# Products of keys and x four at a time in 64x64 tiles of the array, in two stretches a batch

## The chip, the cores and the metric

The program runs on one core of one Trainium2 chip. The time is the device time of one execution in microseconds. The kernel before took 803.41 us in the median of three runs (803.13, 803.41 and 806.71).

A core has five instruction streams that run side by side, each in its own order: TensorE (PE: matrix products; loading its weights is listed apart as PEld), VectorE (DVE), ScalarE (ACT), GpSimd (POOL) and SyncE (SP, which here only issues transfers). They meet at semaphores. Transfers (DMA) are issued by SP, and for v and z by POOL.

## The reference, cut to what matters

Two stages over 8 batches of 3200 rows, 256 wide. The first is a gated attention without softmax:

```
attn = maximum(z @ z.T / 3200, 0) ** 2
x    = u * (attn @ v)                       # per batch 3200 x 256
```

The second mixes rows through a hidden width of 64. As an outer product over rows, it needs no 3200 x 3200 matrix:

```
wq, wk = x @ w_q, x @ w_k                   # 3200 x 64 each
W_tok  = wq @ wk.T / 8
mixed  = W_tok @ x  =  wq @ (wk.T @ x) / 8
out    = maximum(mixed, 0) @ w_out
```

The change is about `wk.T @ x`, a sum over all 3200 rows of a batch that gives 64 x 256 numbers. The kernel calls wk the keys and this product the heads.

## The kernel before, in words

The kernel takes a batch's 3200 rows in 25 tiles of 128, and these in seven groups: six of four tiles (512 rows) and one of a single tile (`LASTG`). For each group it makes

- scores (`scores`, line 223): two row tiles at a time, with 64 rows of contraction each, so that one product uses the upper and the other the lower half of the array;
- their relu (`first_stage`, on DVE line 246 or ACT line 242) and square (`second_stage`, on POOL line 261 or ACT line 259). Because z @ z.T is symmetric, part of the squares is transposed by DMA (line 281) instead of being computed again;
- the second product with v (`second_product`, line 302), the bulk of TensorE's work: 10,000 matmuls with 64 rows of contraction, again one on each half of the array, summed in four PSUM banks (`acc`);
- the gate (`gate`): ACT copies one half's sum into `both` (line 318), DVE adds the other (line 319), POOL multiplies by u into `x_sb` (line 334), and a DMA transposes x (`turn_x`, line 348).

A group's x then goes through the second stage. `use_keys` runs `projections` (line 365: wq and wk together), ACT casts them to `qk` (line 378), and a DMA transposes `qk` into `kx` (`turn_keys`, line 383), so that keys lie with rows on partitions. Two POOL copies double the keys (`double_keys`, line 395), because `heads` (line 402) loads 128 columns of weights: the 64 keys twice, so that the 64 x 256 result appears on both halves of the partitions, where `mix` wants it. For each of a group's tiles there is one matmul on the upper 64 rows of the array and one on the lower, into two banks. They ride in the same PSUM slot as the projections of a later group, right behind them, and DVE adds both banks into `ha` (line 417). After a batch's last group DVE adds the two parts to `hs` (line 424). Then `mix` (line 430), relu on ACT into `rt` (line 447), `proj` with w_out (line 457, the full 128 rows of the array), scaling on ACT into `fo` (line 485) and the store to memory (line 486).

What sets the order: the kernel is scheduled by hand (`manual_schedule`). A planner at build time keeps a clock for each engine, for SP and for the transfers, with fixed costs, and writes the instructions out in the order that comes from it. Within each engine this order is final. `acc` work fills TensorE; everything else (scores, keys, heads, mix, proj) is slipped in when one of two PSUM slots (`ps`, two banks each) is free. `move` hands a transfer to SP with a ready and a due time; `at_time` runs something when the planner's clock gets there.

At the end of the run the last two groups of the last batch are not projected first: their part of the heads comes from x.T @ x (`last_gram`, line 500, and `last_heads`, line 510), and is added to the rest (lines 952 and 959) before the last batch's `mix`.

Of the kernel before, what the change touches and what calls it, by code (L numbers as in the profile page):

```python
# [16 lines left out]
def kernel(  # L17
# [35 lines left out]
    NX = 6  # L53
# [7 lines left out]
    pk = ctx.enter_context(tc.tile_pool(name="pk", bufs=3))  # L61
# [3 lines left out]
    psum = ctx.enter_context(tc.tile_pool(name="psum", bufs=3))  # L65
# [20 lines left out]
    zT, vs, us, xs, xTs, qks, ks, hacc, hss, rts, zds = ({} for _ in range(11))  # L86
# [274 lines left out]
    def projections(b, gi, ps, stop=True):  # L361
        n = min(2, widths[gi] // P)
        for c in range(NC):
            for r in halves(gi):
                nc.tensor.matmul(  # L365
                    out=ps[:, r, 0 : n * P],
                    lhsT=wqk[top(r), c, :, :].rearrange("p t h -> p (t h)"),
                    rhs=xTs[b, gi][top(r), 0:n, c, :],
                    start=(c == 0),
                    stop=(stop and c == NC - 1),  # L370
                )
# [16 lines left out]
    doubled = set()  # L388

    def double_keys(b, gi):  # L390
        doubled.add((b, gi))
        nn = widths[gi] // P
        for r in halves(gi):
            sl = slice(2 * r, min(2 * r + 2, nn))
            nc.gpsimd.tensor_copy(out=ks[b, gi][:, sl, r, :], in_=ks[b, gi][:, sl, 1 - r, :])  # L395

    def heads(b, gi, ps, begun=()):
        nn = widths[gi] // P
        assert (b, gi) in doubled
        for n in range(nn):  # L400
            for r in range(2):
                nc.tensor.matmul(  # L402
                    out=ps[:, r, D : 2 * D],
                    lhsT=ks[b, gi][top(r), n, :, :].rearrange("p a h -> p (a h)"),
                    rhs=x_rows(b, gi, n)[top(r), :, :],
                    start=(n == 0 and r not in begun),
                    stop=(n == nn - 1),
                )
        del xs[b, gi]

    def heads_out(b, gi, ps):
        part = ps[:, 0:2, D : 2 * D]
        if gi == 0:
            hacc[b] = psml.tile([P, 2, D], FP32, tag="ha", name="ha")
            nc.vector.tensor_copy(out=hacc[b][:], in_=part)
        else:
            nc.vector.tensor_add(out=hacc[b][:], in0=part, in1=hacc[b][:])  # L417
# [113 lines left out]
    keys_at, out_of, turned_at, z_at = {}, {}, {}, {}  # L531
# [88 lines left out]
    def double(b, gi):  # L620
        keys_at[b, gi] = give(POOL, clock[PE], 0.6) + 0.5
        double_keys(b, gi)

    def use_keys(b, gi):
        open_slot()
        ps = ps_tile("qk")
        prior = None
        if keyed and keys_at.get(keyed[0], 1e9) <= clock[PE]:
            prior = keyed.pop(0)
        projections(b, gi, ps, stop=not prior)  # L630
        clock[PE] += 0.44 if gi < LASTG else 0.24
        if prior:
            heads(*prior, ps, halves(gi))
            clock[PE] += 0.44 if prior[1] < LASTG else 0.11
# [6 lines left out]
            lambda t: at_time(t, lambda: double(b, gi)),  # L641
        )
        if prior:
            heads_out(*prior, ps)
            done = give(DVE, done, 0.7)
            if prior[1] == LASTG:
                done += 0.4
# [5 lines left out]
        if (b, gi) == (last, LASTG - 2):  # L653
            for _ in keyed:
                add_extra(done + 4.0, "heads", use_heads)

    def use_heads():
        open_slot()
        ps = ps_tile("hd")
        prior = keyed.pop(0)  # L660
        heads(*prior, ps)
        clock[PE] += 0.44 if prior[1] < LASTG else 0.11
        heads_out(*prior, ps)
        done = give(DVE, clock[PE] + FROM_PE, 0.7)
        if prior[1] == LASTG:
            heads_known(prior[0])
        close_slot(done)

# [197 lines left out]
    while groups or work or current["left"]:  # L866
# [9 lines left out]
                and (x[1] != "keys" or len(keyed) < 2 or keys_at.get(keyed[0], 1e9) <= now)  # L876
                and (x[1] != "proj" or len(stored) < 2 or stored[-2] <= now)
                and (x[1] != "heads" or keys_at.get(keyed[0], 1e9) <= now)
# [26 lines left out]
    while extras or later or moves:  # L905
        x = next((x for x in extras if x[1] == "proj"), None)
        if not x:
            ripe = [
                x
                for x in extras  # L910
                if x[1] not in ("keys", "heads")
                or (x[1] == "keys" and len(keyed) < 2)
                or keyed[0] in doubled
            ]
            ripe += [x for x in moves if not x[6] or x[6]()]
            x = min(later + ripe, key=lambda x: x[0])
# [9 lines left out]
    while keyed:  # L926
        use_heads()
# [22 lines left out]
    hsum = psml.tile([P, D], FP32, tag="hm", name="hm", bufs=1)  # L950
    ha = hacc.pop(last)
    nc.vector.tensor_add(out=hsum[:], in0=ha[:, 0, :], in1=ha[:, 1, :])
# [6 lines left out]
    nc.vector.tensor_add(out=hss[last][:], in0=psl[:, 0:D], in1=hsum[:])  # L959
# [45 lines left out]
```

## Time and profile before

| | |
|---|---|
| median of the runs shown | 803.41 us |
| profiled execution: its span, the only time given for it | 804.1 us |
| TensorE busy | 774.2 us (96%), 12,373 matmuls |
| POOL busy | 627.2 us (78%) |
| ACT busy | 579.3 us (72%) |
| DVE busy | 467.7 us (58%) |
| transfers | 141.54 MB, 309,356 packets |

A row of a group of instructions gives line, engine, operation, output and inputs, shapes and count, then the busy time and the mean duration of one, then the idle time of the engine just before them. A row of the timeline gives the start in us, the length in us of the run of like instructions, the engine, and in brackets how long the engine had been idle and whom it waited for. Matmuls overlap: one lasts 0.27 us from its start to the end of its last result, while the next start much sooner. What a matmul costs TensorE is therefore the distance from start to start, which a long run of like matmuls gives.

### The profile page before, as it was taken

The page shows a single profiled execution, that of the slowest core. Times are in us where ns is not written, and L with a number is a line of the kernel's source. Part 1 is how long each engine was busy: PE and PEld are TensorE (multiplying, and loading weights), DVE is VectorE, ACT ScalarE, POOL GpSimd, SP SyncE. Part 2 cuts the span into 40 slices and gives each one's busy share as a digit, 9 for nine tenths or more (in the row PEclk, how much of TensorE's full clock was granted, in tenths as well). Part 3 has the DMA queues.
Part 4 walks back from the last instruction along what each step waited for, and adds up shares of the span by engine and source line. Part 5 has one row for each costly group of instructions (what it writes and reads, how often), then busy time and mean ns, then how long its engine had stood idle before and what let it go on. Part 6 is the DMA issues. An engine that isn't in the chain of part 4 may idle for free.

```text
span 804.1 us, 28204 instructions
## 1 busy us (share of the span) xinstructions
PE 774.2 (96%) x12373; PEld 657.3 (82%) x12373; DVE 467.7 (58%) x485; ACT 579.3 (72%) x690; POOL 627.2 (78%) x512
## 2 busy tenths in 40 slices
PE   7989999997999999999999999999999999999985
PEld 4879899886888888988888788988889788888863
DVE  4665567553666556755576555765557655564424
ACT  5766888774896777877676768777777676887714
POOL 7887878875788878898878878878877887888730
PEclk9999999999999999999999999999999999999998
DMA  7999999999999988999999989999799998787425
GB/s 188 149 159 174 179 179 156 163 170 192 196 160 206 222 159 166 160 219 196 188 161 186 197 173 200 170 193 201 183 179 162 195 220 165 152 165 171 120 48 216
DMA packets 309356, 141.54 MB, mean 176 GB/s; under 512 B 287728, under 2 KB 290672, under 8 KB 309232
## 3 DMA queue, kind: packets, MB, share of 16 engines
q1 hardware_dynamic: 302320, 123.55, 80.4%
q0 software_dynamic: 6768, 15.98, 14.8%
q8 instruction: 97, 1.59, 0.9%
q14 instruction: 27, 0.22, 0.1%
q10 hardware_dynamic: 144, 0.20, 0.1%
HBM read 59.64 MB, written 26.21 MB: 107 GB/s over the span
## 4 chain that ended last, share of the span: by engine, by line
PE 89%; DVE 4%; DMA 2%; ACT 2%; issue 1%; POOL 1%; POOLq 0%; SPq 0%; DVEq 0%; ACTq 0%
PE acc L302 64%; PE sc L223 12%; PE fo L457 6%; PE qk L365 3%; PE qk L402 2%; DVE g L246 2%; PE mx L430 1%; DMA out_dram<-fo 1%; DMA v_sb<-in_v_dram 1%; DVE hs L424 1%; DVE ha L417 1%; POOL at L261 1%; DVE both L319 1%; ACT both L318 0%; DMA z<-in_z_dram 0%
## 5 line engine op out<-in xcount | busy, mean ns | idle before, releaser
L302 PE MATMUL acc<-v_sb,at 64*128 64x256 f16 x7312 | 495.9, 270 | 4.1 <-DVE both L319 2.5
L261 POOL TENSOR_TENSOR at<-g 128x1024 f16<-128x1024 f32 (+1 forms) x238 | 442.7, 1872 | 72.6 <-DVE g L246 63.3
L302 PEld LDWEIGHTS <-at 64*128 64x128 f16 x7312 | 394.2, 94 | 65.3 <-issue 10.8
L246 DVE TENSOR_SCALAR g<-sc 128x1024 f32<-128x1024 f32 (+1 forms) x285 | 333.9, 1189 | 132.9 <-PE sc L223 118.8
L259 ACT ACTIVATE at<-g 128x1024 f16<-128x1024 f32 (+2 forms) x230 | 233.9, 1026 | 16.6 <-DVE g L246 13.0
L242 ACT ACTIVATE g<-sc 128x1024 f32<-128x1024 f32 x183 | 184.9, 1012 | 60.4 <-PE sc L223 59.3
L334 POOL TENSOR_TENSOR x_sb<-both,u_sb 128x512 f16<-128x512 f32 (+1 forms) x112 | 134.5, 1206 | 72.4 <-DVE both L319 70.4
L223 PE MATMUL sc<-zT 64*128 64x512 f16 x920 | 178.5, 379 | 4.6 <-DVE g L246 3.9
L302 PE MATMUL acc<-v_sb,tt 64*128 64x256 f16 x2304 | 162.2, 269 | 0.0
L319 DVE TENSOR_TENSOR both<-acc,both 128x512 f32<-128x512 f32 (+1 forms) x104 | 69.2, 670 | 136.3 <-ACT both L318 131.4
L302 PEld LDWEIGHTS <-tt 64*128 64x128 f16 x2304 | 123.9, 94 | 11.7 <-issue 0.2
L318 ACT COPY both<-acc 128x512 f32<-128x512 f32 (+1 forms) x104 | 58.1, 564 | 42.8 <-PE acc L302 40.9
L223 PEld LDWEIGHTS <-zT 64*128 64x128 f16 x920 | 57.7, 94 | 18.6 <-issue 14.8
L485 ACT ACTIVATE fo<-fo 128x1024 f32<-128x1024 f32 (+2 forms) x50 | 45.4, 909 | 34.1 <-PE fo L457 27.6
L447 ACT ACTIVATE rt<-mx 128x1024 f16<-128x1024 f32 (+1 forms) x49 | 45.7, 934 | 23.1 <-PE mx L430 23.0
L378 ACT CAST qk<-qk 128x512 f16<-128x512 f32 (+1 forms) x54 | 29.4, 545 | 36.7 <-PE qk L402 28.1
L457 PE MATMUL fo<-wo,rt 128*128 128x256 f16 x400 | 53.4, 274 | 1.2 <-ACT rt L445 0.6
L457 PEld LDWEIGHTS <-rt 128*128 128x128 f16 x400 | 34.7, 98 | 15.8 <-issue 9.8
L417 DVE TENSOR_TENSOR ha<-qk,ha 128x512 f32<-128x512 f32 x38 | 26.2, 690 | 33.2 <-ACT qk L378 33.0
L365 PE MATMUL qk<-xT_sb,wqk 64*128 64x256 f16 (+1 forms) x404 | 32.1, 265 | 0.0
L402 PE MATMUL qk<-x_sb,kx 64*128 64x256 f16 x368 | 29.6, 269 | 0.0
L395 POOL COPY kx<-kx 128x128 f16<-128x128 f16 (+1 forms) x101 | 26.1, 288 | 3.0 <-DMA kx<-qk 3.0
(44 smaller groups left out, 225.4 us busy)
## 6 DMA issues: line engine op xcount, KB each, us to landing
u_sb<-in_u_dram SPq DMA_DIRECT2D x48, 512.0 KB, 4.8
out_dram<-fo SPq DMA_DIRECT2D x45, 512.0 KB, 4.8
v_sb<-in_v_dram POOLq DMA_DIRECT2D x35, 320.0 KB, 6.1
zn<-in_z_dram POOLq DMA_DIRECT2D x7, 400.0 KB, 5.9
tt<-at SPq DMA_TRANSPOSE x144, 4.2
out_dram<-fo SPq DMA_DIRECT2D x6, 256.0 KB, 2.1
u_sb<-in_u_dram SPq DMA_DIRECT2D x8, 128.0 KB, 3.3
out_dram<-fo SPq DMA_DIRECT2D x8, 128.0 KB, 2.5
```

The costliest lines, as they stand in the source:

```text
L223: nc.tensor.matmul(out=sc[:, h, 0:gw], lhsT=zT[b][top(h), ts(ti, P)], rhs=zT[b][top(h), ds(gs, gw)], start=True, stop=True,)
L242: nc.scalar.activation(out=g[:, hs, 0:w], in_=sc[:, hs, 0:w], func=RELU, scale=GSCALE)
L246: nc.vector.tensor_scalar(out=g[:, hs, 0:w], in0=sc[:, hs, 0:w], scalar1=0.0, scalar2=GSCALE, op0=AOP.max, op1=AOP.mult,)
L259: nc.scalar.square(out=out, in_=g[:, hs, 0:w])
L261: nc.gpsimd.tensor_mul(out=out, in0=g[:, hs, 0:w], in1=g[:, hs, 0:w])
L302: nc.tensor.matmul(out=accs[half, r][:, ds((j % 2) * D, D)], lhsT=weights(b, gi, ti, j)[top(r), :], rhs=vs[b][top(r), ti, :], start=(first ...
L318: nc.scalar.copy(out=both[:, 0 : n * D], in_=accs[half, 0][:, 0 : n * D])
L319: nc.vector.tensor_add(out=both[:, 0 : n * D], in0=accs[half, 1][:, 0 : n * D], in1=both[:, 0 : n * D])
L334: nc.gpsimd.tensor_mul(out=xs[b, gi][:, 0:n, :, r, :].rearrange("p n c d -> p (n c) d"), in0=both[:, 0 : n * D].rearrange("p (m d) -> p m ...
L365: nc.tensor.matmul(out=ps[:, r, 0 : n * P], lhsT=wqk[top(r), c, :, :].rearrange("p t h -> p (t h)"), rhs=xTs[b, gi][top(r), 0:n, c, :], st ...
L447: nc.scalar.activation(out=out, in_=ps[:, 0:nr, 0 : ND * n * P], func=RELU)
L457: nc.tensor.matmul(out=banks[r][:, ds(j * D, D)], lhsT=flat[:, ds((dc * n + j) * P, P)], rhs=wo[:, dc, :], start=(dc == 0 and j == 0), sto ...
```

## The change

- `heads` multiplies the 64 keys only once: the weights are 64 rows by 64 columns. Even tiles of the stretch write partitions 0 to 63 of the result, odd tiles partitions 64 to 127; in each case one matmul takes the upper and one the lower 64 rows. Four matmuls in a row thus name four different quarters of the array. There are as many matmuls as before (390), each with 256 columns of x.
- Heads no longer ride behind projections. They run in a PSUM slot of their own, in two stretches a batch: one for groups 0 to 2 (24 matmuls), one for groups 3 to 6 (26; in the last batch groups 3 and 4, 16). `keys_landed` starts a stretch when the keys of all its groups are there by the planner's clock.
- `double_keys` and its 101 POOL copies are gone.
- The sum is now split: even tiles on the upper partitions, odd tiles on the lower, two banks each. DVE copies the first stretch's banks to `ha`, adds the second stretch's, and adds the two banks (lines 406, 409 and 410 of the new kernel). Two transfers of 64 x 256 numbers (64 KB each) on SP's queue then carry each half of the partitions to the other (`cross_heads`), and DVE adds what arrives (`heads_done`): for the last batch in place, to be used by the last addition to `hs`.
- `mix` of a batch is planned from the moment at which the crossed halves have landed.
- Buffers: x 7 instead of 6, keys 5 instead of 3, `both` 2 instead of 3; a transposition of keys is issued only while one of the five is free.

The rest of the order is worked out anew by the planner.

```diff
-    NX = 6
+    NX = 7
+    NK = 5
-    pk = ctx.enter_context(tc.tile_pool(name="pk", bufs=3))
+    pk = ctx.enter_context(tc.tile_pool(name="pk", bufs=NK))
-    psum = ctx.enter_context(tc.tile_pool(name="psum", bufs=3))
+    psum = ctx.enter_context(tc.tile_pool(name="psum", bufs=2))
...
-    def double_keys(b, gi):
-        doubled.add((b, gi))
-        nn = widths[gi] // P
-        for r in halves(gi):
-            sl = slice(2 * r, min(2 * r + 2, nn))
-            nc.gpsimd.tensor_copy(out=ks[b, gi][:, sl, r, :], in_=ks[b, gi][:, sl, 1 - r, :])
-
-    def heads(b, gi, ps, begun=()):
-        nn = widths[gi] // P
-        assert (b, gi) in doubled
-        for n in range(nn):
+    def heads(b, gis, ps):
+        todo = [(gi, n) for gi in gis for n in range(widths[gi] // P)]
+        for i, (gi, n) in enumerate(todo):
             for r in range(2):
                 nc.tensor.matmul(
-                    out=ps[:, r, D : 2 * D],
-                    lhsT=ks[b, gi][top(r), n, :, :].rearrange("p a h -> p (a h)"),
+                    out=ps[top(i % 2), r, 0:D],
+                    lhsT=ks[b, gi][top(r), n, 1 - n // 2, :],
                     rhs=x_rows(b, gi, n)[top(r), :, :],
-                    start=(n == 0 and r not in begun),
-                    stop=(n == nn - 1),
+                    start=(i < 2),
+                    stop=(i >= len(todo) - 2),
                 )
...
+    def heads_out(b, ps):
+        if b not in hacc:
+            hacc[b] = psml.tile([P, 2, D], FP32, tag="ha", name="ha", bufs=1)
+            nc.vector.tensor_copy(out=hacc[b][:], in_=ps[:, :, 0:D])
         else:
-            nc.vector.tensor_add(out=hacc[b][:], in0=part, in1=hacc[b][:])
-        if gi == LASTG:
-            heads_done(b)
+            ha = hacc[b]
+            nc.vector.tensor_add(out=ha[:], in0=ps[:, :, 0:D], in1=ha[:])
+            nc.vector.tensor_add(out=ha[:, 0, :], in0=ha[:, 0, :], in1=ha[:, 1, :])
+
+    def cross_heads(b, r):
+        if r == 0:
+            hx[b] = psml.tile([P, D], FP32, tag="hx", name="hx", bufs=1)
+        nc.sync.dma_start(out=hx[b][top(r), :], in_=hacc[b][top(1 - r), 0, :])
 
     def heads_done(b):
-        hss[b] = psml.tile([P, D], FP16, tag="hs", name="hs")
-        ha = hacc.pop(b)
-        nc.vector.tensor_add(out=hss[b][:], in0=ha[:, 0, :], in1=ha[:, 1, :])
+        if b < B - 1:
+            hss[b] = psml.tile([P, D], FP16, tag="hs", name="hs")
+            nc.vector.tensor_add(out=hss[b][:], in0=hacc.pop(b)[:, 0, :], in1=hx.pop(b)[:])
+        else:
+            ha = hacc[b]
+            nc.vector.tensor_add(out=ha[:, 1, :], in0=ha[:, 0, :], in1=hx.pop(b)[:])
...
+    FIRST_HEADS = range(3)
+
+    def keys_landed(b, gi):
         keyed.append((b, gi))
-        if len(keyed) == 2 and gi == LASTG:
-            add_extra(done + 14.0, "heads", use_heads)
+        for gis in FIRST_HEADS, range(3, NG if b < last else LASTG - 1):
+            if gi in gis and all((b, i) in keyed for i in gis):
+                add_extra(clock[PE] + 0.5, "heads", lambda gis=gis: use_heads(b, gis))
+
+    def use_heads(b, gis):
         open_slot()
         ps = ps_tile("hd")
-        prior = keyed.pop(0)
-        heads(*prior, ps)
-        clock[PE] += 0.44 if prior[1] < LASTG else 0.11
-        heads_out(*prior, ps)
+        heads(b, gis, ps)
+        clock[PE] += 0.2 + 0.0547 * sum(widths[gi] // P for gi in gis)
+        heads_out(b, ps)
         done = give(DVE, clock[PE] + FROM_PE, 0.7)
-        if prior[1] == LASTG:
-            heads_known(prior[0])
         close_slot(done)
+        if gis is FIRST_HEADS:
+            return
+        done = give(DVE, done, 0.35)
+        move(done + SLACK, done + 2.0, 0.55, 0.1, lambda: cross_heads(b, 0))
+        move(
+            done + SLACK, done + 2.0, 0.55, 0.1, lambda: cross_heads(b, 1),
+            lambda t: at_time(t, lambda: crossed(b)),
+        )
+
+    def crossed(b):
+        heads_done(b)
+        give(DVE, clock[PE], 0.35)
+        if b < last:
+            heads_known(b)
```

More of the change, by code (lines that the diff above doesn't have):

```diff
@@ L84 @@
     ctx.enter_context(tc.manual_schedule())
-    zT, vs, us, xs, xTs, qks, ks, hacc, hss, rts, zds = ({} for _ in range(11))
+    zT, vs, us, xs, xTs, qks, ks, hacc, hx, hss, rts, zds = ({} for _ in range(12))
     def rows(t, b):
@@ L369, in projections @@
                     start=(c == 0),
[L370 removed]
+                    stop=(c == NC - 1),
                 )
@@ L626, in use_keys @@
         ps = ps_tile("qk")
-        prior = None
-        if keyed and keys_at.get(keyed[0], 1e9) <= clock[PE]:
-            prior = keyed.pop(0)
-        projections(b, gi, ps, stop=not prior)
+        projections(b, gi, ps)
         clock[PE] += 0.44 if gi < LASTG else 0.24
-        if prior:
-            heads(*prior, ps, halves(gi))
-            clock[PE] += 0.44 if prior[1] < LASTG else 0.11
         ready = clock[PE] + FROM_PE
@@ L907 @@
         if not x:
[L908 to L916, printed above, removed]
+            ripe = [x for x in moves if not x[6] or x[6]()]
+            x = min(later + extras + ripe, key=lambda x: x[0])
         clock[PE] = max(clock[PE], x[0])
```

39 lines of the change are left out of this document (6 added, 33 removed).

## The prediction

> **What bounds the kernel now.** I read the page first, then TensorE's waits, the chain of work that ended last, and timeline windows. The page's head and the chain by engine:
>
> ```profile
> span 804.1 us, 28204 instructions
> PE 774.2 (96%) x12373; PEld 657.3 (82%) x12373; DVE 467.7 (58%) x485; ACT 579.3 (72%) x690; POOL 627.2 (78%) x512
> PE 89%; DVE 4%; DMA 2%; ACT 2%; issue 1%; POOL 1%; POOLq 0%; SPq 0%; DVEq 0%; ACTq 0%
> q1 hardware_dynamic: 302320, 123.55, 80.4%
> ```
>
> TensorE is busy almost all the time and carries 89% of the chain. Its longest waits (total, times, longest) are few:
>
> ```profile
> PE mx L430 <- ACT fo L485: 4.5, 1, 4.5
> PE sc L223 <- DVE g L246: 3.9, 6, 1.0
> PE hd L402 <- POOL kx L395: 2.9, 1, 2.9
> ```
>
> So work taken from TensorE's stream between start and tail should shorten the span one for one, and work taken from POOL or DVE should not. Three rows of the chain give a batch and a matmul:
>
> ```profile
> 247.76 1.97 PE acc L302 x36
> 342.96 1.97 PE acc L302 x36
> 761.36 11.73 PE acc L302 x213
> ```
>
> The first two are the same place in two batches: one batch takes 95.2 us, over some 12373/8 = 1547 matmuls, 0.0616 us each with all waits. The third: (11.73 - 0.27)/212 is close to 0.054 us a 64-row matmul, so 0.109 a pair on the two halves of the array (0.0545 below).
>
> **The heads before, and a change of tiling.** A window of the timeline near the end:
>
> ```profile
> 746.21 1.05 PE L457 MATMUL fo<-wo,rt 128*128 128x256 f16 x8
> 747.19 0.39 PE L302 MATMUL acc<-v_sb,at 64*128 64x256 f16 x4
> 756.12 1.91 PE L302 MATMUL acc<-v_sb,tt 64*128 64x256 f16 x32
> 757.96 0.39 PE L457 MATMUL fo<-wo,rt 128*128 128x256 f16 x2
> 758.29 0.61 PE L365 MATMUL qk<-xT_sb,wqk 64*128 64x256 f16 x8
> 758.74 0.60 PE L402 MATMUL qk<-x_sb,kx 64*128 64x256 f16 x8
> 759.17 0.38 PE L302 MATMUL acc<-v_sb,at 64*128 64x256 f16 x4
> ```
>
> Eight head matmuls take 759.17 - 758.74 = 0.43 us, at the usual rate, with no loss on either side. A change to the full array and back costs something: eight fo take 0.98, two take 0.33, so each is 0.108 and the way back 0.11; the way there is 1.84 - 32 x 0.0545 = 0.10. The 64x64 tiles are a tiling that the trace doesn't show. For their change I take the nearest rows, 0.10 each way. Bounds: 0 (only columns are divided anew) and 0.21 each way, twice what is shown.
>
> **TensorE's sum.** Up to the last keys of the last batch, the heads before are 7 x 25 + 12 = 187 pairs: 187 x 0.109 = 20.4 us. After, the same 374 matmuls run in 15 stretches. If four share the time of two now, that is 93.5 rounds x 0.109 = 10.2; if not at all, 20.4. The nearest evidence is the pair: two 64-row matmuls of 256 columns take what one fo of 128 rows takes (0.109 against 0.108), so independent parts of the array run together without loss. I take 10.2. The changes of tiling add 15 x 2 x 0.10 = 3.0 (0 to 6.3). Net -7.2 us; ends -10.2 and +6.3.
>
> Against the full gain speaks the loading of weights, one load for each matmul:
>
> ```profile
> L402 PEld LDWEIGHTS <-kx x390: 92/94/136, 79.9 to 779.2; 64*128 64x128 f16 x195
> 784.48 0.30 PEld L510 LDWEIGHTS hl<-G,wk 128*128 128x128 f32 x2 [0.94 <-ACT G L955]
> L510 PEld LDWEIGHTS hl<-G,wk x4: 186/188/189, 783.2 to 784.6; 128*128 128x128 f32 x4
> ```
>
> The f32 loads last 188 ns against 94, and the second begins 0.30 - 0.19 = 0.11 us behind the first. If 64-column loads went at that slower rate, each would occupy 0.055: two behind each other for each half of the rows fit a round of 0.109; four behind each other make it 0.22. The Trainium skill, "TensorEngine Tiling (Array Packing)", Restrictions, says that column tiling disables the fast weight load; "TensorE: Matmul & The Clock Gate", LDWEIGHTS, gives columns / 1.2 GHz for a load, 53 ns for 64. By those rules with one path for all loads, the sum would be the second rival's. No run shows a 64-column load; the f32 row agrees with the rate.
>
> **Off TensorE.** Rows of the costliest groups:
>
> ```profile
> L246 DVE TENSOR_SCALAR g<-sc 128x1024 f32<-128x1024 f32 (+1 forms) x285 | 333.9, 1189 | 132.9 <-PE sc L223 118.8
> L417 DVE TENSOR_TENSOR ha<-qk,ha 128x512 f32<-128x512 f32 x38 | 26.2, 690 | 33.2 <-ACT qk L378 33.0
> L395 POOL COPY kx<-kx 128x128 f16<-128x128 f16 (+1 forms) x101 | 26.1, 288 | 3.0 <-DMA kx<-qk 3.0
> ```
>
> POOL loses 26.1 us. DVE loses 54 operations of 0.69 for 16 such and some of half the size, and in the new order takes 26 more relus of 1.2 from ACT, which evens out. All three stay under 80% busy and hidden behind TensorE: nothing. Projections no longer hold their slot for DVE's addition; the 3.9 us of waits for slots is all that this could give, and 16 extra slots take some back: nothing net. `both` with two buffers waits for the products of the gate before last; at the tightest place (the tail below) POOL ends them at 773.72 and ACT copies at 776.12: nothing while those 2.4 us hold.
>
> The 16 crossing transfers are 1 MB beside 141.5 and 16 issues on SP, in front of transpositions queued behind them. Prices of an issue and a landing come from 64 KB loads:
>
> ```profile
> L183 SPq DMA_DIRECT2D wk<-in_moe_w_k_dram x4: 472/606/1438, 21.5 to 35.8; - x4
> DMA to landing us min/median/max: 2.4/3.0/6.5
> ```
>
> Two issues delay SP by 1.2 us a batch, within what a transposition has in hand (rival three). DVE's last addition stands some 90 to 200 matmuls (5.5 to 12 us) behind the crossing in the written order, against a landing of 3.0: hidden, except in the tail, and at 6.5 a DVE wait of 1 us, with relu work queued behind it.
>
> **The tail.** The last keys hold up the end:
>
> ```profile
> 771.95 1.77 POOL L334 TENSOR_TENSOR x_sb<-both,u_sb 128x512 f16<-128x512 f32 x1 [7.43 <-DVE both L319]
> 774.72 1.19 SPq L383 DMA_TRANSPOSE kx<-qk  x1
> 776.01 4.37 SPq L348 DMA_TRANSPOSE xT_sb<-x_sb  x2
> 776.12 0.37 ACT L318 COPY both<-acc 128x256 f32<-128x256 f32 x1 [1.43 <-PE acc L302]
> 777.03 1.64 POOL L334 TENSOR_TENSOR x_sb<-both,u_sb 128x256 f16<-128x256 f32 x2 [1.34 <-DVE both L319]
> 778.62 0.52 POOL L395 COPY kx<-kx 128x128 f16<-128x128 f16 x2
> 778.97 0.86 PE L402 MATMUL hd<-x_sb,kx 64*128 64x256 f16 x8 [2.93 <-POOL kx L395]
> 783.25 0.70 PE L510 MATMUL hl<-G,wk 128*128 128x256 f32 x2 [0.19 <-DVE G L954]
> ```
>
> Without the earlier heads the cast starts 0.44 sooner, and without copies the heads start when keys land: at 776.6 to 778.0 (landing 2.3 to 3.6 after 774.72, less 0.44) instead of 778.97. But DVE must then add twice (1.1 us), the crossing waits on SP behind the last transposition of x, issued by about 780, and lands 3.0 later, near 783.5; and DVE's copy for the last product with w_k is queued behind the addition that waits for it, two operations of some 0.4 (a little over half of 0.69, for half the size): 784.3 instead of 783.25. I take +1.0; ends -1.0 (the crossing hidden) and +3.0 (it lands last behind both transpositions).
>
> **One stall.** The single long wait, in the second batch:
>
> ```profile
> 180.34 8.14 DMA out_dram<-fo
> 188.56 0.38 ACT L485 ACTIVATE fo<-fo 128x256 f32<-128x256 f32 x1 [6.39 <-DMA out_dram<-fo]
> 188.99 0.61 PE L430 MATMUL mx<-qk,hs 64*128 64x256 f16 x4 [4.51 <-ACT fo L485]
> 189.37 2.57 PE L302 MATMUL acc<-v_sb,at 64*128 64x256 f16 x22
> ```
>
> A scaling waits 6.39 us for its buffer, as the store is late, and TensorE waits 4.51. Then 22 matmuls take 2.57 instead of 1.4, mx 0.38 instead of 0.22, with the next ones slow too: some 6.1 in all. In the new order the stores of that batch are queued 148 or more matmuls ahead of the scaling that needs the buffer, against 138 here: 0.6 us more, not 6.39. I keep the stall.
>
> **The sum.** 804.1 - 20.4 + 10.2 + 3.0 + 1.0 = 797.9. The profiled execution is 0.7 above the median 803.4, so 797.2. Its own ends, with a change of tiling at 0 to 0.15 us and the tail at -1 to +3: 792.2 to 800.7.
>
> **Rivals.** (1) The stall goes too: the batch's mix comes later, so stores meet other transfers. 797.2 - 6.1 = 791.1. For it: it happens in one batch of seven. Against: the early loads, and a margin hardly larger.
>
> (2) Slower: four loads go one behind the other. Rounds of 0.22 give 93.5 x 0.22 = 20.6, nothing is saved, and changes and tail stay: 804.1 + 0.2 + 3.0 + 1.0 - 0.7 = 807.6. It decides from a round of 0.174 on, where (20.4 - 4.0)/93.5 is used up. Speaking for it is the f32 row; against it, that pairs run together. The plainer form, that the quarters don't run together, ends at the same time.
>
> (3) TensorE waits for keys. Formerly they lay ready for a group; now each stretch follows its last transposition by as little as 108 matmuls (6.6 us), ten of them by under 8 us. Landing is:
>
> ```profile
> L383 SPq DMA_TRANSPOSE kx<-qk x54: 1182/1254/2805, 61.9 to 774.7; - x54
> DMA to landing us min/median/max: 2.3/4.0/7.7
> ```
>
> At the median 2.6 us are in hand, at 7.7 none. Behind TensorE stand acc matmuls that need none of it. With 0.5 us on average at ten places: 802.2. At 0.6 a place the gain is gone.
>
> **How the numbers follow.** A measurement of this kernel can tell about 0.5% (4 us) from no change: faster ends below 799.4, slower begins at 807.4. Forecast 0.48 (0.44 faster, 0.04 same). Stall gone 0.22 (faster). Loads in a row 0.14 (0.07 same, 0.07 slower, as 807.6 sits on the bound). Waits for keys 0.16 (0.02 faster, 0.11 same, 0.03 slower). Faster 0.68, same 0.22, slower 0.10. The range takes in the stall's going and the waits, and leaves out most of rival two: 789.5 to 805.0.
>
> **What would show it.** Right: 24 head matmuls take 0.65 to 0.7 us, four starting together every 0.11, with 0.1 lost at either end; a batch takes 94.2 instead of 95.2; the tail from keys to the w_k product is about 1 us longer. Wrong: rounds of 0.2; rows where hd waits for kx, or DVE for hx; a wait of mx or fo for a store, new or gone.

## The result

The new kernel takes 792.04 us in the median (790.96 to 793.60, four runs) against 805.06 us for the old one beside it (803.13 to 807.06, four runs): ratio 0.987, interval 0.983 to 0.992. It is faster, by 1.3%. On another chip, where both were run again more often, it took 792.77 us (six runs) against 800.96 (17 runs, 797.9 to 805.3): ratio 0.990, interval 0.987 to 0.993. The old kernel varies more from run to run than the new one, and the first chip caught it at the long end. The gain to be explained is therefore 8 us rather than 13; the forecast was 6.2 us (797.2 against 803.4, a ratio of 0.992).

Head of the page of the new kernel, and its chain by engine. Its profiled execution took 790.96 us of device time with a span of 789.2; that of the old one had a span of 804.1.

```profile
span 789.2 us, 28159 instructions
PE 763.2 (97%) x12373; PEld 645.7 (82%) x12373; DVE 479.4 (61%) x479; ACT 551.8 (70%) x659; POOL 612.9 (78%) x418
PE 91%; DVE 3%; DMA 2%; issue 1%; ACT 1%; POOL 1%; SPq 0%; DVEq 0%; POOLq 0%; ACTq 0%
```

TensorE has as many matmuls as before and is busy 11.0 us less. POOL has 94 instructions fewer. Three of TensorE's waits (total, times, longest):

```profile
PE hl L509 <- DVE G L936: 5.1, 1, 5.1
PE sc L224 <- DVE g L247: 3.1, 5, 0.8
PE hd L393 <- DMA kx<-qk: 0.6, 1, 0.6
```

The 4.5 us in which `mx` waited for a store are gone. In their place the tail has a wait of 5.1 us for `G`, where a wait of 2.9 us for the key copies stood. Waits for keys, the third rival, come to 0.6 us, once, in the tail.

Two stretches of heads in TensorE's timeline, with the row that follows each:

```profile
378.92 0.85 PE L393 MATMUL hd<-x_sb,kx 64*64 64x256 f16 x24
379.70 1.05 PE L456 MATMUL fo<-wo,rt 128*128 128x256 f16 x8
...
419.91 0.95 PE L393 MATMUL hd<-x_sb,kx 64*64 64x256 f16 x26
420.80 0.39 PE L303 MATMUL acc<-v_sb,at 64*128 64x256 f16 x4
```

From the start of a stretch to the start of what follows, 24 matmuls take 0.78 us and 26 take 0.89. At the old rate of 0.0545 a matmul they would have taken 1.31 and 1.42. The single records show why: four matmuls start 3 to 4 ns apart, and the next four begin 0.099 us after the last of them, 0.123 us the first time. Taken over the 15 stretches, the last matmul ahead of a stretch is 0.093 us longer than the last of a pair usually is, and the last of a stretch 0.096 longer than the last of four: that is the change of tiling.

The weight loads, first in the new kernel and then in the old (count, then busy time and mean ns of one):

```profile
L303 PEld LDWEIGHTS <-at 64*128 64x128 f16 x7312 | 393.0, 94 | 66.8 <-issue 12.7 <-ACT g L243 2.0
L393 PEld LDWEIGHTS <-kx 64*64 64x64 f16 x390 | 9.7, 106 | 4.6 <-issue 3.7 <-DMA kx<-qk 0.9
```

```profile
L402 PEld LDWEIGHTS <-kx 64*128 64x128 f16 x390 | 21.3, 94 | 4.6 <-POOL kx L395 3.2
```

A load of 64 columns lasts 106 ns, longer than one of 128 columns with 94. But 390 x 0.106 = 41 us of loads fill only 9.7 us of time: some four go on at once. In the old kernel 390 x 0.094 = 37 us filled 21.3, not quite two at once.

**Where the time went.** Between 60 us from the span's start and the start of the last `acc` matmul I summed two things over TensorE's records: the time from the start of each head matmul to the start of the next matmul, and all that the other matmuls took beyond their usual distance (acc 0.0547, sc 0.108, qk and mx 0.054, fo 0.109). The second sum holds waits, slow clock and changes of tiling; the ways into the head stretches, 15 x 0.093 = 1.4 us, are in it.

| profiled execution | heads, us | all else beyond the usual, us |
|---|---|---|
| before | 21.0 | 24.1 |
| before, two more profiles | 21.0, 21.0 | 22.9, 20.3 |
| after | 12.4 | 17.8 |
| after, once more | 12.6 | 17.7 |

Heads and their ways in go from 21.0 to 13.8, so -7.2 us; 0.4 of that is eight matmuls that now stand behind the last `acc` matmul. All else goes from 24.1 to 16.4, so -7.7 us. From the last `acc` matmul to the end it is 28.29 before and 28.45 after, +0.16. Together -14.7 of the 14.9 us between the two spans. The forecast had the first, and +1.0 for the third; for the second it had nothing.

### The profile page after: what moved, and what is told of

Same layout as the page of the kernel before. It is cut to its first block, busy times and chain, and to the rows that moved or that the text cites. A ratio compares the mean times of both kernels' runs of the same rounds, so it can differ in the third digit from the quotient of the medians.

```text
span 789.2 us, 28159 instructions
## 1 busy us (share of the span) xinstructions
PE 763.2 (97%) x12373; PEld 645.7 (82%) x12373; DVE 479.4 (61%) x479; ACT 551.8 (70%) x659; POOL 612.9 (78%) x418
## 4 chain that ended last, share of the span: by engine, by line
PE 91%; DVE 3%; DMA 2%; issue 1%; ACT 1%; POOL 1%; SPq 0%; DVEq 0%; POOLq 0%; ACTq 0%
PE acc L303 66%; PE sc L224 12%; PE fo L456 6%; PE qk L366 3%; DVE g L247 2%; PE hd L393 1%; PE mx L429 1%; DVE both L320 1%; DMA v_sb<-in_v_dram 1%; DMA hx<-ha 1%; ACT both L319 1%; POOL x_sb L335 1%; DVE ha L410 0%; DMA z<-in_z_dram 0%; SPq L349 0%
## 5 line engine op out<-in xcount | busy, mean ns | idle before, releaser
L262 POOL TENSOR_TENSOR at<-g 128x1024 f16<-128x1024 f32 (+2 forms) x245 | 451.5, 1858 | 82.5 <-DVE g L247 66.5
L247 DVE TENSOR_SCALAR g<-sc 128x1024 f32<-128x1024 f32 (+2 forms) x309 | 363.9, 1197 | 153.0 <-PE sc L224 137.6
L260 ACT ACTIVATE at<-g 128x1024 f16<-128x1024 f32 x223 | 229.4, 1036 | 30.7 <-DVE g L247 27.2
L243 ACT ACTIVATE g<-sc 128x1024 f32<-128x1024 f32 (+1 forms) x159 | 159.2, 1003 | 60.5 <-PE sc L224 59.8
L303 PE MATMUL acc<-v_sb,tt 64*128 64x256 f16 x2304 | 158.7, 269 | 0.0
L224 PEld LDWEIGHTS <-zT 64*128 64x128 f16 x920 | 56.8, 94 | 17.6 <-issue 12.4
L366 PEld LDWEIGHTS <-wqk 64*128 64x128 f16 x416 | 22.8, 94 | 2.5 <-issue 0.5
L303 PE MATMUL acc<-v_sb,ttl 64*128 64x256 f16 x384 | 24.6, 269 | 0.0
L303 PEld LDWEIGHTS <-ttl 64*128 64x128 f16 x384 | 19.7, 94 | 3.5 <-issue 0.8
```

What stands on the lines that cost most here:

```text
L224: nc.tensor.matmul(out=sc[:, h, 0:gw], lhsT=zT[b][top(h), ts(ti, P)], rhs=zT[b][top(h), ds(gs, gw)], start=True, stop=True,)
L243: nc.scalar.activation(out=g[:, hs, 0:w], in_=sc[:, hs, 0:w], func=RELU, scale=GSCALE)
L247: nc.vector.tensor_scalar(out=g[:, hs, 0:w], in0=sc[:, hs, 0:w], scalar1=0.0, scalar2=GSCALE, op0=AOP.max, op1=AOP.mult,)
L260: nc.scalar.square(out=out, in_=g[:, hs, 0:w])
L262: nc.gpsimd.tensor_mul(out=out, in0=g[:, hs, 0:w], in1=g[:, hs, 0:w])
L303: nc.tensor.matmul(out=accs[half, r][:, ds((j % 2) * D, D)], lhsT=weights(b, gi, ti, j)[top(r), :], rhs=vs[b][top(r), ti, :], start=(first ...
```

## The experiments: do the four quarters run together?

**One half of the columns at a time (e8).** The first stretch of a batch writes only the upper 64 partitions of the result, the second only the lower. The number of matmuls, stretches and changes of tiling stays; the two quarters of the other column half are idle.

```diff
-                    out=ps[top(i % 2), r, 0:D],
+                    out=ps[top(gis[0] > 0), r, 0:D],
...
-                    start=(i < 2),
-                    stop=(i >= len(todo) - 2),
+                    start=(i == 0),
+                    stop=(i == len(todo) - 1),
...
-            nc.vector.tensor_copy(out=hacc[b][:], in_=ps[:, :, 0:D])
+            nc.vector.tensor_copy(out=hacc[b][top(0), :, :], in_=ps[top(0), :, 0:D])
...
-            nc.vector.tensor_add(out=ha[:], in0=ps[:, :, 0:D], in1=ha[:])
+            nc.vector.tensor_copy(out=ha[top(1), :, :], in_=ps[top(1), :, 0:D])
```

> The new kernel, in which the first stretch of a batch uses only the left column half of the array and the second only the right one, so that there is never a matmul for more than two quarters at hand; DVE copies what each stretch gives to its half of the partitions, the rest is the same, and every engine but DVE keeps its order. If it is the four quarters at once that save time, a stretch of 24 takes 1.2 us from first to last start instead of 0.58, and the kernel 10 us more than the new one. If not, it takes the same as the new one.

It took 799.90 us (797.11 to 801.86, 10 runs) against 800.96 for before: 0.998, interval 0.996 to 1.000. That is 7.1 us more than the new kernel on the same chip; nearly the whole gain is gone. The stretch of 24 in its timeline:

```profile
383.27 1.50 PE L393 MATMUL hd<-x_sb,kx 64*64 64x256 f16 x24
384.70 1.05 PE L456 MATMUL fo<-wo,rt 128*128 128x256 f16 x8
```

1.43 us to the next matmul instead of 0.78. The heads' sum is 22.2 us instead of 12.6, while all else is 16.0 instead of 17.7. So it is the four quarters at once that save TensorE's time on heads. The two stretches, their changes of tiling, their new places and the missing copies are all still there in e8; together they leave it 1.1 us under before, which is not clear of nothing. I expected 10 us more and got 7.1; in the profiled execution, the longest of the ten, the span is 9.9 us above that of the new kernel on this chip (800.1 against 790.2).

**Even tiles first, then odd ones (e1).** All matmuls of one column half stand in the program ahead of all of the other, so that neighbours never name four quarters.

```diff
-        for i, (gi, n) in enumerate(todo):
+        turns = [x for x in enumerate(todo) if x[0] % 2 == 0] + [x for x in enumerate(todo) if x[0] % 2]
+        for i, (gi, n) in turns:
```

> The new kernel, in which each stretch of heads runs all its even tiles first and then all its odd ones: the same matmuls, sums and changes of tiling, but only two quarters of the array have work at a time. If the gain is that four quarters run together, a stretch of 24 goes from 0.58 us (first to last start) to about 1.25, and all stretches up to the last keys cost some 10 us more: about 802 against 792 for the new kernel. If the quarters are not what makes it shorter (the gain lies in fewer waits, or in heads that no longer hold a slot), the stretches stay as short and the time stays at 792.

It took 794.21 us (793.17 to 795.48, five runs), 0.992 of before with an interval of 0.989 to 0.995. It did not keep the quarters apart as meant, so the time expected, 802, did not come:

```profile
379.82 1.09 PE L394 MATMUL hd<-x_sb,kx 64*64 64x256 f16 x24
380.85 1.05 PE L457 MATMUL fo<-wo,rt 128*128 128x256 f16 x8
```

1.03 us, between 0.78 and 1.43. In one stretch of 24 the starts of the single matmuls fall into two series of six pairs, each pair some 0.11 us behind the last of its series: one from 186.027 to 186.597, the other from 186.279 to 186.849. The second series begins when the first is at its third pair, though the program has the odd tiles behind all even ones. So, read from the starts (a record does not name its quarter), the matmuls of the free column half overtook those in front of them, and two thirds of the matmuls of a stretch had a partner in the other half all the same. The heads' sum is 16.2 us.

**Six stretches a batch (e7).** One stretch for each group (the last two together, and in the last batch five stretches), with the x buffers back at 6 and two `ha`. Here the order is worked out anew.

```diff
+        ends = [[0], [1], [2], [3], [4]] + ([[5, 6]] if b < last else [])
-        for gis in FIRST_HEADS, range(3, NG if b < last else LASTG - 1):
+        for gis in ends:
```

> The new kernel with the heads group by group instead of in two stretches: six stretches in a batch (the single-tile group goes with the sixth), 47 in all instead of 16, with the same 390 matmuls (x has six buffers, ha two; the planner works the order out anew). If each stretch costs 0.19 us for the two changes of tiling, as the new kernel's profile shows, that is 5.9 us more on TensorE, and DVE has 31 more additions, which are hidden: about 798 to 799 against 792.8. If a change of tiling is hidden or much cheaper, under 2 us.

It took 803.00 us (799.99 to 811.36, 10 runs) against 801.39: 1.002, interval 0.998 to 1.006. The gain is gone, with four quarters in use. A stretch of eight and what follows, and its waits for score slots:

```profile
367.67 0.41 PE L393 MATMUL hd<-x_sb,kx 64*64 64x256 f16 x8
368.01 0.39 PE L224 MATMUL sc<-zT 64*128 64x512 f16 x2
```

```profile
PE sc L224 <- DVE g L247: 6.2, 8, 1.7
```

Eight matmuls take 0.34 us where 8 x 0.0545 = 0.44 would be the old way, and a way in of 0.093 comes on top: nothing is left of the saving in so short a stretch. Against the new kernel heads and ways in cost some 7 us more in the profiles (31 more stretches at 0.19, and slower first rounds). The expectation had 5.9 of it, and 798 to 799 in all. The rest of the 10 us is waits, and a granted clock of 0.5 for 3.4 us; how much of that belongs to the new order and the x buffers, and not to the shorter stretches, this run does not separate. That the stretches are long is a condition of the gain.

## The experiments: what else became shorter?

**Before, twice more (e9).** The kernel before without a change (in the second, a comment is added).

> The kernel before, profiled again. If the 4.5 us wait of mx behind a late store in the second batch belongs to the kernel, it is in this profile too and the second batch takes 100 us; if it is chance, the wait is absent or short, the second batch takes about 95 and the span is about 798, as with three buffers.

> The same a second time: where chance decides, the two profiles may differ; where the kernel decides, both show the wait.

They took 802.17 and 801.15 us. The wait for the late store, in the first and in the second:

```profile
PE mx L430 <- ACT fo L485: 2.2, 1, 2.2
```

```profile
PE mx L430 <- ACT fo L485: 0.6, 1, 0.6
```

With the 4.5 us of the first profile that is three sizes from one program. The stall is there each time, at the same place. Its length goes with the time that the scaling waits for the store: 6.4, 4.0 and 2.5 us. In the longer two the granted clock then fell to 0.5 for 3.4 us, which made the first one worth 6.1 us. Stretch 165 to 200 us, before (the first profile) and then after (columns: stretch, its length, busy time and instructions of each engine, granted clock, share and GB/s of DMA):

```profile
165.00:200.00 35.00, 30.49 (x470) 24.33 (x472) 14.00 (x16) 19.45 (x25) 22.61 (x18) 0.95 1.05 177
```

```profile
165.00:200.00 35.00, 34.87 (x574) 28.80 (x572) 17.76 (x20) 21.81 (x28) 25.93 (x19) 1.00 1.05 207
```

**Before, without the stall, in two ways (e2, e4).** e2 gives `fo` a third buffer, and pays for the room with one `ha` and two buffers of `both`; each engine's order stays. e4 has the planner begin `mix` later.

```diff
-            fo = pg.tile([P, 2, W], FP32, tag="fo", name="fo", bufs=2)
+            fo = pg.tile([P, 2, W], FP32, tag="fo", name="fo", bufs=3)
```

```diff
-                    add_extra(t + 4.0 + 18.0 * i, "mix", lambda gi=gi: use_mix(b, gi))
+                    add_extra(t + 15.5 + 18.0 * i, "mix", lambda gi=gi: use_mix(b, gi))
```

> The kernel before with three buffers for fo instead of two; every engine's order stays the same (the room comes from both with two buffers and ha with one, as in the new kernel). If the long wait in the second batch is for a store's buffer and nothing else, TensorE's wait of mx for fo (4.5 us) is gone with the slow clock behind it, and the time falls by about 6: 799 against 805. If the lateness of stores and transpositions only comes to light at the next place, a wait of another kind appears in the second or third batch, and the time stays at 803 to 805.

> The kernel before, with mix planned 15.5 us instead of 4.0 behind the heads, so about where the new kernel has it in a batch; heads as before. If the stall went because mix and stores come later, the wait of a scaling for its store is gone in the second batch and the time falls by about 6, to 799. If the place of mix is not the cause, the wait is there again (3 us or more) and the time is 803 to 806.

e2 took 800.53 us (1.001 of before, interval 0.998 to 1.004), e4 801.92 (1.002, 0.999 to 1.005). In neither profile does `mx` wait for a store, and neither is faster than before. At most 1.8 us of a usual run are to be had from the stall by e2 (0.22% at the lower end of its interval); the buffers that e2 gave up do not show among TensorE's waits, which are 2.5 us for `both` in either. Both expectations, about 799 by a fall of 6, miss: before itself was at 800.2 on that chip. The 6.1 us that I carried through the whole forecast were one execution's.

**The copies put back (e3, e10).** The new kernel, with the 101 copies on POOL as before; nothing reads what they write. In e3 the planner does not know of them, and the other engines keep their order; in e10 it plans 0.6 us of POOL for each group (the line with `give`).

```diff
+    def double_keys(b, gi):
+        nn = widths[gi] // P
+        for r in halves(gi):
+            sl = slice(2 * r, min(2 * r + 2, nn))
+            nc.gpsimd.tensor_copy(out=ks[b, gi][:, sl, r, :], in_=ks[b, gi][:, sl, 1 - r, :])
...
     def keys_landed(b, gi):
+        double_keys(b, gi)
+        give(POOL, clock[PE], 0.6)
```

> The new kernel with the 101 POOL copies of keys put back at the places at which the keys land (nothing reads what they write); the other engines' orders stay the same. If the long wait in the second batch went because POOL, rid of 26 us of copies, frees x and squares for SP's queue earlier, the wait comes back and the time rises by 4 to 6, to about 797. If it went because the order changed (mix and stores come later in the batch), the time stays within 1.5 of 792 and the copies cost nothing.

> The new kernel with the 101 POOL copies back, and this time the planner is told of them (0.6 us of POOL for each group's keys), so that it can give squares to ACT instead; nothing reads the copies. In the run where it was not told, the span was 4.5 us above the new kernel's, with TensorE waiting for relus on DVE that waited for POOL's buffers. If that loss comes from the plan being off, it shrinks to under 1.5 here. If POOL's time itself is what TensorE pays for, it stays at 3 to 5.

e3 took 796.03 us (793.35 to 799.13, 10 runs), 0.994 of before (0.992 to 0.997); e10 796.39 (789.88 to 801.35, 10 runs), 0.994 (0.990 to 0.998). The new kernel stood at 0.990: 3.3 to 3.7 us less than both. For e3 the runs lie nearly apart from the new kernel's 791.98 to 794.44; e10's enclose them, so its difference is not clear of noise. In e3's table of groups, and among its waits:

```profile
L393 POOL COPY kx<-kx 128x128 f16<-128x128 f16 x94 | 24.7, 293 | 1.9 <-DMA kx<-qk 1.9
```

```profile
PE sc L224 <- DVE g L247: 5.8, 6, 1.5
```

The 25 us of copies do not show as a wait for POOL. They show as `sc` waiting 5.8 us instead of 3.1 for DVE's relu, which empties a score slot. That relu stands in DVE's order behind the addition of the two banks. One of these places, DVE and then TensorE, in the new kernel and then in e3:

```profile
515.49 1.85 DVE L410 TENSOR_TENSOR ha<-ha 128x256 f32<-128x256 f32 x1
518.52 0.39 PE L224 MATMUL sc<-zT 64*128 64x512 f16 x2 [0.76 <-DVE g L247]
```

```profile
519.53 2.47 DVE L416 TENSOR_TENSOR ha<-ha 128x256 f32<-128x256 f32 x1
523.19 0.39 PE L224 MATMUL sc<-zT 64*128 64x512 f16 x2 [1.38 <-DVE g L247]
```

Where POOL is idle, this addition of two operands in SBUF (on-chip memory) takes 0.43 us. In four batches it lasts 1.58 to 1.85 us in the new kernel and 2.37 to 2.47 in e3, and each of the eight ends 0.28 to 0.30 us behind the end of a POOL instruction. In e3 one more instruction, a copy of 0.23 us, stands among POOL's at each of the four, and the addition lasts through more of POOL's work. So it seems to wait for POOL; what the two contend for was not tested. The four waits of `sc` behind it grow by 0.89, 0.63, 0.62 and 0.55 us: that is the whole difference of 2.7. All else in the table above goes from 17.7 to 21.5 us, so about 1 us is not explained by this. The time rose although the stall did not come back, which neither side of e3's expectation had.

e10 loses its time elsewhere. Its profiled execution is the longest of its ten:

```profile
PE mx L435 <- ACT fo L490: 6.2, 2, 3.2
PE sc L224 <- DVE g L247: 2.1, 4, 0.8
```

`sc` waits less than in the new kernel. But `mx` waits for a store again, in two batches, and POOL itself stands 15.3 us at copies whose keys have not landed (1.9 in e3). So e10 does not show that POOL's time is what TensorE pays for, though its median lies where that was expected; and as e3 has no stall, the copies alone do not bring it back.

**After, once more (e0).** The reference for the second group of runs.

> The new kernel itself once more, beside the kernel before on the same chip: it measures the ratio where the long wait for a store may or may not be in the runs of before. The earlier group of runs had before at 800.2 in the median (796 to 808), where the first had 805.1. If the stall is a matter of chance of the run, new against before comes out at 0.989 to 0.990 here (a gain of 8 to 9 us); if it is in every run of before, again at 0.987.

792.77 us (791.98 to 794.44), with the same waits. So the new kernel's time repeats.

## The experiments: the tail

The forecast put DVE's copy of `G` behind the addition that waits for the crossing. TensorE in the tail of the new kernel, then DVE and SP's queue there (the row of `kx` is the last keys):

```profile
758.73 2.28 PE L303 MATMUL acc<-v_sb,ttl 64*128 64x256 f16 x37
760.94 0.41 PE L393 MATMUL hd<-x_sb,kx 64*64 64x256 f16 x8
761.97 0.41 PE L393 MATMUL hd<-x_sb,kx 64*64 64x256 f16 x8 [0.61 <-DMA kx<-qk]
...
769.48 2.07 PE L509 MATMUL hl<-G,wk 128*128 128x256 f32 x4 [5.15 <-DVE G L936]
```

```profile
759.59 1.19 SPq L384 DMA_TRANSPOSE kx<-qk  x1
...
761.12 4.75 SPq L349 DMA_TRANSPOSE xT_sb<-x_sb  x2
...
763.15 0.78 DVE L410 TENSOR_TENSOR ha<-ha 128x256 f32<-128x256 f32 x1
...
765.96 1.18 SPq L415 DMA_DIRECT2D hx<-ha  x2
768.66 0.43 DVE L423 TENSOR_TENSOR ha<-ha,hx 128x256 f32<-128x256 f32 x1 [4.73 <-DMA hx<-ha]
769.01 0.42 DVE L936 COPY G<-xtx 128x256 f32<-128x256 f32 x1
```

The chain is the one foreseen. The heads' sums are ready at 763.93; the crossing stands on SP's queue until 765.96 behind the second transposition of x; DVE waits 4.73 us in the addition, and the copy of `G`, whose data has long been there, waits with it. From the start of the last `acc` matmul (758.73 + 2.28 - 0.27 = 760.74) to `hl` it is 8.74 us, against 783.25 - 775.76 = 7.49 before: +1.25.

**The addition behind the copy (e5).** In the last batch alone DVE adds `hx` after it has copied `G`.

```diff
-        else:
-            ha = hacc[b]
-            nc.vector.tensor_add(out=ha[:, 1, :], in0=ha[:, 0, :], in1=hx.pop(b)[:])
...
     nc.scalar.copy(out=g32[:, D : 2 * D], in_=psg[:, D : 2 * D])
+    ha = hacc[last]
+    nc.vector.tensor_add(out=ha[:, 1, :], in0=ha[:, 0, :], in1=hx.pop(last)[:])
```

> The new kernel with one DVE instruction moved at the end: the addition that waits for the crossed halves of the last batch comes behind the copy of x.T x instead of ahead of it. If TensorE's wait of 5.1 us ahead of the last product with w_k is that copy queued behind the crossing, the product starts about 5 us earlier after the last acc matmul (3.8 instead of 8.7) and the span falls by 4 to 5. If the crossing itself sets the end (the last mix needs it anyway), the wait moves to that mix, and the gain is under 1.

It took 788.07 us (787.12 to 788.81, four runs): 0.984 of before (0.980 to 0.987), and 4.7 us less than the new kernel on the same chip. It beats both kernels. Its tail:

```profile
765.59 0.42 DVE L933 COPY G<-xtx 128x256 f32<-128x256 f32 x1
766.07 0.70 PE L506 MATMUL hl<-G,wk 128*128 128x256 f32 x2 [0.19 <-DVE G L933]
767.48 1.18 SPq L415 DMA_DIRECT2D hx<-ha  x2
770.17 0.42 DVE L936 TENSOR_TENSOR ha<-ha,hx 128x256 f32<-128x256 f32 x1 [4.16 <-DMA hx<-ha]
```

`hl` starts before the crossing is even issued. From the last `acc` matmul to `hl` it is now 3.79 us, to the end 23.07 instead of 28.45. DVE's wait is nearly as long as before (4.16 against 4.73), but what stands behind it is now only what needs it.

**And the crossing on another queue (e6).** As e5, and the last batch's two transfers are issued by ACT.

```diff
-        nc.sync.dma_start(out=hx[b][top(r), :], in_=hacc[b][top(1 - r), 0, :])
+        queue = nc.sync if b < B - 1 else nc.scalar
+        queue.dma_start(out=hx[b][top(r), :], in_=hacc[b][top(1 - r), 0, :])
```

> As the run with the addition moved, and the last batch's two crossing transfers go out on ACT's queue instead of SP's, where they stand behind two transpositions of x. If after the move the crossing is next to set the end, this gives 1 to 2 us more than the move alone; if the matmuls of the end set it, it gives nothing more.

It took 789.95 us (787.41 to 792.00, four runs), 0.987 of before (0.983 to 0.991): nothing over e5.

```profile
762.06 1.94 ACTq L416 DMA_DIRECT2D hx<-ha  x2
762.60 0.70 PE L507 MATMUL hl<-G,wk 128*128 128x256 f32 x2 [0.19 <-DVE G L934]
765.70 0.43 DVE L937 TENSOR_TENSOR ha<-ha,hx 128x256 f32<-128x256 f32 x1 [3.15 <-DMA hx<-ha]
765.87 0.38 ACT L935 COPY G<-xtx 128x256 f32<-128x256 f32 x1
766.30 1.22 PE L507 MATMUL hl<-G,wk 128*128 128x256 f32 x2 [2.99 <-ACT G L935]
```

The transfers leave at once, and the addition comes sooner. But issuing them keeps ACT from 762.06 to 764.00, then two relus follow, 1.94 us together, and ACT's half of `G` comes only at 765.87: the second pair of `hl` waits 2.99. The wait has moved to another engine.

## Why the prediction was right, and where it was not

**TensorE bounds the kernel: right.** It carries 91% of the chain after, and what the heads lost came out of the span (e8 gives it back).

**Four quarters in the time of two: right.** Forecast 20.4 to 10.2 for 374 matmuls, with 3.0 for changes of tiling: -7.2. By the records, eight stretches of (0.782 + 0.093) and seven of (0.884 + 0.093) make 13.84, so -6.6. The change of tiling, taken as 0.10 each way from the nearest rows, measured 0.093 in and 0.096 out. The missing 0.6 us lies in rounds that are not four full ones: the first of a stretch takes 0.134 instead of 0.109, and 26 matmuls need seven rounds.

**Rival two, four loads in a row: refuted.** A 64-column load is slow, as the f32 row hinted: 106 ns, twice the 53 that the prediction quotes. What was wrong in the rival is that loads take turns: 41 us of them fit into 9.7. The Trainium skill, "TensorEngine Tiling (Array Packing)", says under Restrictions that column tiling disables the fast weight load, and under Key Properties that tiles load and multiply in parallel and that a change of tiling drains the array. The trace agrees with all three: 106 ns against 94, four loads at once, and 0.19 us for a change there and back.

**Rival three, waits for keys: hardly.** 0.6 us in the tail, and in e5 once 1.5 us in another batch. Stretches come late enough after the last transposition.

**"All three stay ... hidden behind TensorE: nothing": wrong for POOL.** The copies' 26.1 us were priced at nothing because POOL was 78% busy and off the chain. Put back in e3, they cost 3.3 to 3.7 us. This is a term that was put at nothing and has a price. What failed is the step from "off the chain" to "free": beside POOL's instructions an addition on DVE gets longer, the next relu comes later, and a score slot with it (2.7 us in e3). The prediction took the old kernel's 3.9 us of waits for slots as a matter of slots; 2.5 of it stands behind line 424's addition, which lasts 1.63, 1.63 and 1.44 us there instead of 0.43. What the copies cost in the old order, whose plan counts with them, no run shows, as its heads read them.

**"I keep the stall": wrong.** No profile of the new kernel has it. But what its absence is worth was mis-sized too: the same program shows 4.5, 2.2 and 0.6 us, and e2 and e4 without it were no faster. So the first rival, at 791.1 the nearest number to the 792.0 measured, was right about the stall's going, and would have been right by its sum only for executions like the first profile. Why the new order is free of it isn't settled: e3 shows that it isn't the absence of the copies alone, and e10 shows it again with another order.

**The tail: the mechanism right, the sum by luck.** +1.0 was forecast, +1.05 for `hl`, of which the trace has +1.25. Two things came that I hadn't listed. One is the clock. Windows of the tail, before and then after:

```profile
779.00:783.20 4.20, 4.05 (x26) 1.62 (x26) 1.54 (x3) 0.97 (x2) 0.14 (x1) 0.59 0.17 31
```

```profile
769.40:772.90 3.50, 3.42 (x14) 2.34 (x16) 0.45 (x2) 0.83 (x2) 0.00 (x0) 0.56 0.00 0
```

Behind the wait of 5.15 us the granted clock is 0.56 while `hl` and the first `fo` run; before, it was 0.59 behind the wait of 2.93, while `xtx` ran. The other is the very end, where the last stores land sooner. The stores of the tail, before and then after (duration of an issue in ns and time to landing, each least, median, most):

```profile
L486 SPq DMA_DIRECT2D out_dram<-fo x12: 332/332/1312, 786.3 to 799.5; - x12
...
DMA to landing us min/median/max: 2.0/2.9/4.5
```

```profile
L485 SPq DMA_DIRECT2D out_dram<-fo x12: 332/332/491, 773.1 to 785.7; - x12
...
DMA to landing us min/median/max: 2.0/2.6/2.7
```

From `hl` to the third run of eight `fo` it is 6.24 us before (789.49 - 783.25) and 6.89 after (776.37 - 769.48): +0.65. From the last `fo` run to the end it is 8.11 (804.06 - 795.95) and 6.36 (789.19 - 782.83): -1.75. With +1.25 that makes +0.15. The landing of the crossing was taken as 3.0 us from loads of the same size. In the tail the addition starts 2.7 us after the first of the two issues (768.66 - 765.96), but over all batches the landing was mis-sized:

```profile
L415 SPq DMA_DIRECT2D hx<-ha x16: 492/582/923, 142.8 to 766.6; - x16
...
DMA to landing us min/median/max: 1.9/4.7/7.9
```

Outside the tail that was hidden, as forecast: DVE waited 0.3 us in all for the other seven batches.

**From the span to the median.** I subtracted 0.7 because the first profile's span stood 0.7 above the median of the runs. But an execution takes longer than its span: 1.8 us in the new kernel, and 1.7 to 1.9 in every run here that gives both. By that, as an estimate, the first profile of before is an execution of 805.9 us, a long one.

**What stays open.** Against a usual run of before, heads give -6.6, the tail +0.2, the copies -3.3 to -3.7 and the stall up to -1.8; that is -9.7 to -11.9, where the larger comparison measured -8.2. If these sums hold, 1.5 to 3.7 us of the new order's own costs lie in between. e3, which has the copies but no stall and is 4.1 us faster than before where heads and tail make 6.4, points to 2.3. Neither is clear of noise: the interval of the 8.2 us reaches from 5.8 to 10.5, that of the 4.1 from 2.5 to 6.5. I didn't find their place. So the mechanism of the heads was right, but that the forecast of 6.2 lies near 8.2 is partly luck: the copies and the stall, which it left out, and whatever the new order costs go opposite ways.

## What to carry to other kernels

Products with 64 rows and 64 columns of weights cost half when four of them name four quarters, but every change to that tiling and back costs 0.19 us: group them into long stretches (24 gain 1.31 - 0.78 - 0.09 = 0.44 net, 8 gain nothing). Work on an engine off the chain isn't free when another engine's instructions get longer beside it, as a DVE addition of 0.43 us did here beside POOL (up to 2.47); price it by putting it back or taking it out, and look for the wait that grew. And look at what stands behind an instruction that waits for a transfer: one copy moved ahead of such a wait was worth 4.7 us here, more than half of what the whole change gave.

## What was unexpected in the hardware

Matmuls for idle quarters start ahead of matmuls that the program has before them (e1: 24 in 0.825 us from first to last start, where one column half alone took 1.228 in e8). The Trainium skill, "TensorE: Matmul & The Clock Gate", Part 3, The mechanism, says that matmuls start and end in the order of the program; here the measurement decides, and by their starts they did not.

A DVE addition with both operands in SBUF takes 0.43 us with POOL idle, and up to 1.85 in the new kernel and 2.47 in e3, where it ends 0.3 us behind a POOL instruction. That it waits for POOL is read from these times alone.

In all four further profiles of the old kernel's order or close to it (e2, e4 and e9 twice) one issue among the last stores takes 1.26 to 1.31 us and the last landing 4.5 to 4.6; in all profiles of the new kernel and its variants no such issue is over 0.5 us and no landing over 2.7. No experiment was made on it, and its cause is open.
